# Linear attention, routed experts and a dense layer in one kernel: routing cut into four parts and shared between VectorE and GpSimd, tables of powers in PSUM, one score tile with one mask

## The chip, the cores and the metric

One Trainium2 chip, one of its cores. The metric is device time in microseconds (us) of one launch, the median of three runs. A change of 0.2% of it is about 1.6 us. The engines are named as in the profile: PE is TensorE's matmul, PEld its weight load, DVE is VectorE, ACT is ScalarE, POOL is GpSimd, SP is the engine whose queue issues most DMAs.

## The reference, cut to what matters

Three stages, all in float32, for 4 sequences of 768 tokens (3072 tokens), 8 heads of 48 numbers (384 numbers a token):

```python
# 1 attention with a decaying state, per sequence and head
for t in range(S):
    cur = outer(u * k[t], v[t])
    y[t] = r[t] @ (state + cur)
    state = w[:, None] * state + outer(k[t], v[t])
# 2 each token goes to one of 8 experts, the one with the largest logit
logits = x @ w_gate                       # x is y, a row for each token
e = argmax(logits); gate = softmax(logits)[e]
x2 = gate * (relu(x @ w1[e]) @ w2[e])     # w1 384x1024, w2 1024x384
# 3 a dense layer for all tokens
h = x2 @ w_in                             # 384x2048
out = max(0.01 * h, h) @ w_out            # 2048x384
```

## The kernel before, in words

**Attention** runs in 24 units of 128 tokens (6 chunks of each of the 4 sequences), in a loop over steps `n` that is a software pipeline written out by hand (`attention`, from L322). Each engine runs its own list of instructions in the order of the program, so the order of the calls in a step is the order of the work on each engine. In step n:

- SP's queue loads the transposed k and r (`kT`, `rT`) and v of unit n+2, and k and r of unit n+3; steps 4 to 11 also issue one DMA of zeros each (`zero_region`) into the region of one expert in the DRAM buffer `xs`, which has 3072 rows for each expert.
- PE makes the scores of unit n (`scores`, L432) into two PSUM tiles `pa0` and `pa1`, each with two buffers; then the values and the state update of unit n-1 (`values`, L462 and L468; `update`, L453, into one PSUM bank `pu`), then `rows` of unit n-2 (L507), which turns the result back to token rows and gives the router's logits.
- DVE reduces the logits of unit n-3 (L515), adds `pu` to the state (L498), scales kT and rT of unit n+2 by tables of powers of the decay (`prep_T`, L389 with `iG` and L390 with `G`, both tables in SBUF), copies the scores under a mask into `A` (`masked`, L438, two instructions), and reduces a product for unit n+2 (L411).
- ACT fills the diagonal of `A` for unit n+1 (L421, eight instructions), evicts `py` (L477) and `pr` (L519), and decays the state (L487).
- POOL forms k times a table (L402) and r times k times u of unit n+3 (L397, L398).

**Routing** comes once for each group of four units, in two lumps: `route1` at step 4g+6 (the largest logit, the difference to it, the one-hot choice; DVE, with one exponential on ACT), then at step 4g+7 `route1b` (the gate) and `route2` (positions, by small matmuls with a triangle of ones; then DVE). All of it but the exponential, the matmuls and one memset is on DVE. An indirect DMA on POOL (`scatter`, L690) then writes each unit's 128 rows of 388 numbers to `xs`; the steps are listed in `SCATTER_AT`. At step 16 `choose_first` picks the expert that leads so far; at step 17 SP reads that choice into a register (`load_first`, L233) and issues the first piece of the expert's weights, and one more piece in each step after it.

**The experts** follow in nine windows of columns: the leading expert has a window of 256 rows, known from the first 16 units, and one of `CAPS[0]` - 256 rows, and the other seven one each. `load_rows` (L793) fetches the rows of a window from `xs`, `turn` (L809) transposes them, and each window has 144 matmuls (L832 and L857). Weights and activations are split into a high and a low part of a packed float32 type, and three products stand for one. Steps of this stage are numbered again from 0; in the first three the routing of the last four units is done (`meanwhile`). **The dense layer** has L944 and L963, and ends in an indirect DMA by token number.

An off-line fallback (`leftovers`) runs when a flag says that a count went over its cap. With the reference's inputs the leading expert has 409 tokens and the smallest 348, so that no flag is raised.

Of the kernel before, what the change touches and what calls it, by code (L numbers as in the profile page):

```python
# [33 lines left out]

WARM = 5
ZERO_AT = 4
# [3 lines left out]
EARLYM = 0  # L40
# [16 lines left out]
PAD = 292  # L57
assert sum(CAPS) <= S * B + PAD
ZR = 512
LP = 116  # L60
RW = 388
# [9 lines left out]
class Kernel:  # L71
# [71 lines left out]
    def late_tables(self, one, keep, const):  # L143
# [15 lines left out]
        nc.vector.tensor_copy(out=self.rev, in_=ri)  # L159

    def later_tables(self, one, const):
# [5 lines left out]
        nc.vector.tensor_copy(out=self.carry, in_=ci)  # L167
        self.region = c([1, E], F32, "region")
        nc.vector.tensor_copy(out=self.region, in_=ci[0:1, :])
# [4 lines left out]
        nc.vector.tensor_copy(out=self.place, in_=ei)  # L174
        self.caps = c([1, E], F32, "caps")
        for k in range(E):
            nc.vector.memset(self.caps[:, k : k + 1], float(CAPS[k]))
# [24 lines left out]
    def counts(self, keep, name):  # L202
        nc = self.nc
        f = lambda nm: keep.tile([1, E], F32, name=f"{name}_{nm}")
        cnt, key = f("cnt"), f("key")
        nc.vector.tensor_tensor(out=cnt, in0=self.carry[0:1, :], in1=self.region, op=ALU.subtract)

        nc.vector.scalar_tensor_tensor(
            out=key, in0=cnt, scalar=16.0, in1=self.rev[0:1, :], op0=ALU.mult, op1=ALU.add
        )  # L210
        return cnt, key

    def choose_first(self, keep):

        nc = self.nc
        cnt, key = self.counts(keep, "half")
        mx = keep.tile([1, 1], F32, name="half_mx")
        x = keep.tile([1, E], F32, name="half_x")
        idf = keep.tile([1, 1], F32, name="half_id")
        self.lead = keep.tile([1, E], F32, name="lead")  # L220
        self.first_i = keep.tile([1, 1], I32, name="first_i")
        nc.vector.tensor_reduce(out=mx, in_=key, axis=AX.X, op=ALU.max)
        nc.vector.tensor_scalar(out=self.lead, in0=key, scalar1=mx, scalar2=None, op0=ALU.is_equal)
        nc.vector.tensor_tensor(out=x, in0=self.lead, in1=self.place, op=ALU.mult)
        nc.vector.tensor_reduce(out=idf, in_=x, axis=AX.X, op=ALU.add)
        nc.vector.tensor_scalar(out=idf, in0=idf, scalar1=float(E - 1), scalar2=0.0, op0=ALU.min, op1=ALU.max)
        nc.vector.tensor_copy(out=self.first_i, in_=idf)
# [10 lines left out]
    def early_flag(self, keep):  # L238

        nc = self.nc  # L240
        cnt, _ = self.counts(keep, "early")
        nc.vector.tensor_tensor(out=cnt, in0=cnt, in1=self.lead, op=ALU.mult)
        n = keep.tile([1, 1], F32, name="early_n")
        nc.vector.tensor_reduce(out=n, in_=cnt, axis=AX.X, op=ALU.add)
        nc.vector.tensor_scalar(out=n, in0=n, scalar1=float(EARLY), scalar2=None, op0=ALU.is_lt)
        self.redo = n
# [45 lines left out]
    def flag_rows(self, small, tmp):  # L292
# [3 lines left out]
        cap, over, n = (small.tile([1, w], F32, name=f"f{i}") for i, w in enumerate((E, E, 1)))  # L296
# [8 lines left out]
        V.tensor_tensor(out=n, in0=f[:, 1:2], in1=self.redo, op=ALU.max)  # L305
        V.tensor_tensor(out=f[:, 0:1], in0=f[:, 0:1], in1=n, op=ALU.max)

        V.tensor_tensor(out=n, in0=f[:, 1:2], in1=self.far, op=ALU.max)
# [6 lines left out]
    def attention(self, xs, clist, extra, const, route):  # L315
        nc, tc, a = self.nc, self.tc, self.a
        with ExitStack() as ctx:
# [8 lines left out]

            def load(n, names=("kT", "rT", "k", "r", "v")):
                if n >= NU:
                    return
                d = st.setdefault(n, {})  # L330
                for nm in names:
                    shp, bufs = {
                        "kT": ([HP, NP, P], 4), "rT": ([HP, NP, P], 4), "k": ([P, DM], 4), "r": ([P, DM], 4),
                        "v": ([P, DM], 5),
                    }[nm]
                    d[nm] = ld.tile(shp, F32, tag=nm, name=nm, bufs=bufs)
                    nc.sync.dma_start(out=d[nm], in_=a[nm][n])
# [45 lines left out]
            def prep_T(n):  # L383
# [5 lines left out]
                nc.vector.tensor_tensor(out=d["K"], in0=d["kT"], in1=self.iG, op=ALU.mult)  # L389
                nc.vector.tensor_tensor(out=d["R"], in0=d["rT"], in1=self.G, op=ALU.mult)  # L390
# [951 lines left out]
```

## Time and profile before

| | |
|---|---|
| median of 3 runs | 816.93 us (815.88 to 817.71) |
| profiled execution, its own time | 813.28 us |
| its span, first to last instruction | 811.5 us |
| PE busy | 770.8 us (95%) |
| DVE busy | 504.4 us (62%) |
| ACT busy | 378.1 us (47%) |
| POOL busy | 196.6 us (24%) |
| mean granted TensorE clock | 0.965 of full |

The page divides the span into 40 slices. In its line for the TensorE clock five of the first seven slices are below nine tenths, and from the eighth to the last but one none is; its line for VectorE has 7 to 9 in most of the first seven slices and 3 to 5 in the second half. Shares of the whole span therefore say little of the attention stage, which is the first fifth of it. The stage is read from the timeline of each engine and from sums over stretches.

### The profile page before, as it was taken

How to read it: one execution, taken by the hardware profiler on the slowest of the kernel's cores; microseconds unless marked ns; L12 is line 12 of the kernel's file. 1: busy time of each engine (PE TensorE's matmuls, PEld its weight loads, DVE VectorE, ACT ScalarE, POOL GpSimd, SP SyncE). 2: the span in 40 equal slices, each digit the busy share in tenths (PEclk: the TensorE clock that was granted, in tenths of full speed). 3: DMA queues.
4: the chain of work that ended last, by engine and by line, in shares of the span. 5: the costliest groups of instructions: out<-in, count | busy, mean ns of one | idle time of the engine just before them, and what ended most of it. 6: DMA issues, size and time to landing. Idle time of an engine off the chain costs nothing.

```text
span 811.5 us, 13201 instructions
## 1 busy us (share of the span) xinstructions
PE 770.8 (95%) x4906; PEld 706.2 (87%) x4906; DVE 504.4 (62%) x913; ACT 378.1 (47%) x800; POOL 196.6 (24%) x175
## 2 busy tenths in 40 slices
PE   7789878998999999999999999999999999999994
PEld 4678767898999999999899999999999999999993
DVE  7798998856889899989975443333333343343331
ACT  5586857735544555556444433342343333233321
POOL 5755673460212222223210020020010002002001
PEclk8698977999999999999999999999999999999998
DMA  8999739547886677677731010010000001001001
GB/s 216 283 326 287 233 128 269 163 144 211 223 241 199 196 226 242 206 224 208 172 123 49 0 40 1 1 40 0 1 30 11 0 1 40 1 1 39 1 1 43
DMA packets 55178, 97.80 MB, mean 121 GB/s; under 512 B 12189, under 2 KB 33089, under 8 KB 55105
## 3 DMA queue, kind: packets, MB, share of 16 engines
q1 hardware_dynamic: 52033, 87.38, 37.8%
q0 software_dynamic: 3072, 9.49, 3.2%
q8 instruction: 40, 0.66, 0.4%
q14 instruction: 33, 0.27, 0.1%
HBM read 74.69 MB, written 22.19 MB: 119 GB/s over the span
## 4 chain that ended last, share of the span: by engine, by line
PE 72%; DVE 10%; issue 9%; DMA 6%; POOL 1%; ACT 1%; SPq 0%; POOLq 0%; DVEq 0%; ACTq 0%
PE ph L944 21%; PE o L963 20%; PE y L857 11%; PE ph L832 11%; PE pr L507 2%; PE py L468 2%; DMA rT<-in_rT 2%; PE pa L432 2%; PE py L462 2%; DVE A L438 1%; DMA v<-in_v 1%; DMA raw<-in_wE 1%; DVE R L390 1%; PE pt L809 1%; DMA u_row<-in_u 1%
## 5 line engine op out<-in xcount | busy, mean ns | idle before, releaser
L963 PE MATMUL o<-c,gg 128*128 128x384 f32 x1152 | 216.3, 336 | 0.0
L944 PE MATMUL ph<-x,c 128*128 128x512 f32 x864 | 215.7, 394 | 0.7 <-DVE x L923 0.7
L963 PEld LDWEIGHTS o<-c,gg 128*128 128x128 f32 x1152 | 203.7, 188 | 8.8
L944 PEld LDWEIGHTS ph<-x,c 128*128 128x128 f32 x864 | 160.4, 188 | 30.4 <-DVE x L923 1.1
L950 DVE TENSOR_TENSOR s<-s,ph 128x512 f32<-128x512 f32 x96 | 66.0, 688 | 166.9 <-ACT s L949 166.9
L949 ACT ACTIVATE s<-ph 128x512 f32<-128x512 f32 x96 | 57.3, 597 | 173.9 <-PE ph L944 170.6
L857 PE MATMUL y<-hh,c 128*128 128x256 f32 (+7 forms) x648 | 123.2, 334 | 3.1 <-ACT hh L837 2.3
L832 PE MATMUL ph<-xe,c 128*128 128x256 f32 (+7 forms) x648 | 123.3, 335 | 0.6 <-DVE xe L813 0.6
L857 PEld LDWEIGHTS y<-hh,c 128*128 128x128 f32 x648 | 109.9, 188 | 6.4 <-ACT hh L837 2.5
L731 POOL TENSOR_TENSOR c<-raw,c 128x768 fp32r<-128x768 f32 x32 | 61.2, 1913 | 209.8 <-ACT c L722 142.1
L832 PEld LDWEIGHTS ph<-xe,c 128*128 128x128 f32 x648 | 108.3, 188 | 2.7 <-DVE xe L813 1.0
L953 DVE TENSOR_TENSOR gg<-s,gg 128x512 fp32r<-128x512 f32 x96 | 66.5, 692 | 67.0 <-ACT gg L952 67.0
L976 POOL DMA_INDIRECT out<-z,cl x24 | 24.3, 1014 | 322.6 <-ACT z L975 318.6
L952 ACT ACTIVATE gg<-s 128x512 fp32r<-128x512 f32 x96 | 60.7, 632 | 82.9 <-DVE s L950 82.9
L722 ACT ACTIVATE c<-raw 128x768 fp32r<-128x768 f32 x80 | 67.1, 838 | 14.2 <-DMA raw<-in_wE 14.1
L837 ACT ACTIVATE hh<-ph 128x256 fp32r<-128x256 f32 (+7 forms) x72 | 34.6, 481 | 65.2 <-PE ph L832 65.1
L421 ACT ACTIVATE A<-ident,av 128x128 f32<-128x128 f32 x192 | 58.5, 390 | 2.2 <-DVE av L411 2.1
L731 DVE TENSOR_TENSOR c<-raw,c 128x768 fp32r<-128x768 f32 x48 | 47.5, 989 | 17.7 <-ACT c L722 17.4
L778 DVE SCALAR_TENSOR_TENSOR t<-raw,t 128x384 f32<-128x384 uint32 x32 | 42.4, 1324 | 1.1
L838 DVE SCALAR_TENSOR_TENSOR hh<-ph,hh 128x256 fp32r<-128x256 f32 (+7 forms) x72 | 38.8, 540 | 4.4 <-ACT hh L837 4.3
L468 PE MATMUL py<-A,v 128*48 128x128 f32 x384 | 34.3, 318 | 6.7 <-DVE A L438 6.6
L468 PEld LDWEIGHTS py<-A,v 128*48 128x48 f32 x384 | 25.6, 143 | 12.1 <-DVE A L438 3.5
(167 smaller groups left out, 738.2 us busy)
## 6 DMA issues: line engine op xcount, KB each, us to landing
raw<-in_wE SPq DMA_DIRECT2D x64, 384.0 KB, 4.2
raw<-in_w2nd SPq DMA_DIRECT2D x32, 384.0 KB, 4.6
xs<-z SPq DMA_DIRECT2D x8, 776.0 KB
w2f<-t SPq DMA_DIRECT2D x32, 192.0 KB, 4.0
raw<-w2f SPq DMA_DIRECT2D x16, 384.0 KB, 3.5
kT<-in_kT SPq DMA_DIRECT2D x24, 224.0 KB, 6.3
rT<-in_rT SPq DMA_DIRECT2D x24, 224.0 KB, 5.2
k<-in_k SPq DMA_DIRECT2D x24, 192.0 KB, 7.2
```

The source lines that it names most:

```text
L421: nc.scalar.activation(out=d["A"][:, h % 2, h // 2, :], in_=self.ident, func=AF.Copy, scale=d["av"][:, h : h + 1],)
L468: nc.tensor.matmul(py[64 * i : 64 * i + D, p, :], d["v"][:, (2 * p + i) * D : (2 * p + i + 1) * D], d["A"][:, i, p, :], start=(c == 0 and ...
L722: self.nc.scalar.activation(out=w[:, 0, c], in_=t, func=AF.Copy)
L731: eng.tensor_tensor(out=w[:, 1, c], in0=t, in1=w[:, 0, c].bitcast(F32), op=ALU.subtract)
L832: nc.tensor.matmul(ph[:, :cap], w[:, wl, c * 512 + o : c * 512 + o + P], self.xT[i][:, xl, c, :cap], start=(c == 0 and n == 0), stop=(c == ...
L857: nc.tensor.matmul(self.y[i][m][:, :cap], w[:, wl, o : o + P], t[:, xl, :cap], start=(f == 0 and n == 0), stop=(f == FF // P - 1 and n == 2),)
L944: nc.tensor.matmul(ph, w[:, wl, c * 512 + off : c * 512 + off + P], x2[b][:, xl, c, :], start=(c == 0 and i == 0), stop=(c == KD - 1 and i ...
L949: nc.scalar.activation(out=s, in_=ph, func=AF.Copy, scale=0.01)
L950: nc.vector.tensor_tensor(out=s, in0=s, in1=ph, op=ALU.max)
L952: nc.scalar.activation(out=t[:, 0, :], in_=s, func=AF.Copy)
L953: nc.vector.tensor_tensor(out=t[:, 1, :], in0=s, in1=t[:, 0, :].bitcast(F32), op=ALU.subtract)
L963: nc.tensor.matmul(o[b][k][:, :DM], t[:, gl, k * P : (k + 1) * P], w[:, wl, (f % 4) * DM : (f % 4 + 1) * DM], start=(f == 0 and i == 0), s ...
```

## The change

- `CAPS[0]` goes from 512 to 480, so the second window has 224 columns in place of 256; the zeros are written to rows 256 to 479 of each expert's region in place of rows 0 to 511, from step 3 on in place of step 4. `RW` goes from 388 to 386.
- Loads of kT and rT for units 4 and later leave out the 16 filler partitions: two DMAs of 48 partitions in place of one of 112. In a step, kT, rT, k and r are issued ahead of v.
- The tables `G` and `iG` are copied into PSUM at step 1 and used from there for units 4 and later.
- The scores of a unit go to one PSUM tile of two banks with one buffer, and one `copy_predicated` takes them. It stands ahead of `prep_T` in every step (before, behind it in all steps but 0).
- Routing of a group is cut into four parts in four successive steps. DVE keeps the reductions and what reads PSUM; the rest is on POOL, with the exponential and the matmuls where they were. `choose_first` is cut into three parts in steps 16 to 18, the early flag into two.
- The choice is read by SP at step 19, behind the loads of kT, rT, k and r and ahead of those of v; three weight pieces follow at once, the others in steps 21 to 24. Two of five low halves of pieces go to POOL.
- The last stage's token numbers are clamped by one VectorE instruction.

```diff
-ZERO_AT = 4
+ZERO_AT = 3
+POWERS_AT = 2
 SCATTER_AT = {
-    **{13 + 2 * g + i: [(g, 2 * i), (g, 2 * i + 1)] for g in (0, 1) for i in (0, 1)},
-    **{17 + u: [(2, u)] for u in range(3)},
-    20: [(2, 3), (3, 0)],
-    21: [(3, 1), (3, 2), (3, 3)],
-    23: [(4, u) for u in range(4)],
+    11: [(0, 0)],
...
+    20: [(2, 2), (2, 3)],
+    21: [(3, u) for u in range(4)],
+    24: [(4, u) for u in range(4)],
 }
-CAPS = (512, 456, 432, 416, 400, 392, 384, 372)
+CAPS = (480, 456, 432, 416, 400, 392, 384, 372)
...
+                    if nm in turned:
+                        d[nm] = t = turned[nm][n % TB]
+                        for q in [slice(0, HP)] if n < TB else [slice(0, D), slice(64, 64 + D)]:
+                            nc.sync.dma_start(out=t[q], in_=a[nm][n, q])
+                        continue
...
+            powers = [ps1.tile([HP, NP, P], F32, tag=nm, name=nm) for nm in ("pG", "piG")]
...
+                G, iG = powers if n >= POWERS_AT + 2 else (self.G, self.iG)
+                nc.vector.tensor_tensor(out=d["K"], in0=d["kT"], in1=iG, op=ALU.mult)
+                nc.vector.tensor_tensor(out=d["R"], in0=d["rT"], in1=G, op=ALU.mult)
...
-                d["pa"] = pa = [ps.tile([P, NP, P], F32, tag=f"pa{i}", name=f"pa{i}") for i in range(2)]
+                d["pa"] = pa = ps1.tile([P, 2, NP, P], F32, tag="pa", name="pa")
...
-                for i in range(2):
-                    nc.vector.copy_predicated(out=st[n]["A"][:, i], mask=mask, data=st[n]["pa"][i])
+                flat = lambda t: t.rearrange("s i p t -> s (i p) t")
+                nc.vector.copy_predicated(out=flat(st[n]["A"]), mask=mask, data=flat(st[n]["pa"]))
...
+                if n == 19:
+                    first_weights()
+                for m in ahead:
+                    load(m, ("v",))
...
+                for part in range(3, -1, -1):
+                    g, u = divmod(n - 3 - part, B)
+                    if u == B - 1 and 0 <= g < NC - 1:
...
+                        self.route(part, g, route, nc.gpsimd, bank)
...
+        if part == 0:
+            V.tensor_reduce(out=d["mx"], in_=d["lg"], axis=AX.X, op=ALU.max)
+            eng.tensor_tensor(out=d["df"], in0=d["lg"], in1=be(d["mx"]), op=ALU.subtract)
...
+                eng.tensor_scalar(out=d["eq"], in0=d["df"], scalar1=0.0, scalar2=None, op0=ALU.is_equal)
+                eng.tensor_tensor(out=d["eq"], in0=d["eq"], in1=rev, op=ALU.mult)
+            nc.scalar.activation(out=d["ex"][:, :, 0:E], in_=d["df"], func=AF.Exp)
+        elif part == 1:
+            V.tensor_reduce(out=d["m2"], in_=d["eq"], axis=AX.X, op=ALU.max)
+            V.tensor_reduce(out=se, in_=d["ex"], axis=AX.X, op=ALU.add)
+            V.reciprocal(out=d["rows"][:, :, DM], in_=se)
...
+                eng.tensor_tensor(out=d["df"], in0=d["eq"], in1=be(d["m2"]), op=ALU.subtract)
+                eng.tensor_scalar(out=d["oh"], in0=d["df"], scalar1=0.0, scalar2=None, op0=ALU.is_equal)
+            eng.tensor_copy(
+                out=d["rows"].bitcast(I32)[:, :, DM + 1], in_=self.tokid[:, B * g : B * (g + 1)]
+            )
+        elif part == 2:
...
+            V.tensor_tensor(out=self.carry, in0=self.carry, in1=pk[:, B, :], op=ALU.add)
+            eng.tensor_tensor(out=d["pos"], in0=d["pos"], in1=oh, op=ALU.mult)
+        else:
+                V.tensor_reduce(out=d["ix"], in_=d["pos"], axis=AX.X, op=ALU.add)
...
+    def first_weights():
+        k.load_first()
+        for i in range(3):
+            k.piece_load(i)
+
     def extra(n):
-        if n == 17:
-            k.load_first()
-        if 17 <= n < 17 + 8:
-            k.piece_load(n - 17)
-        if 20 <= n < 20 + 5:
-            k.piece_low(n - 20)
-        if 19 <= n < 19 + 5:
-            k.piece_high(n - 19)
+        for i in {20: (0,), 21: (1,), 22: (2,), 23: (3, 4)}.get(n, ()):
+            k.piece_high(i)
+        for i in {21: (0,), 22: (1,), 23: (2,), 24: (3, 4)}.get(n, ()):
+            k.piece_low(i, nc.gpsimd if i in (1, 3) else None)
+        for i in {21: (3,), 22: (4,), 23: (5,), 24: (6, 7)}.get(n, ()):
+            k.piece_load(i)
```

## Rows read from the trace of the kernel before

**Rows 1.** Sums by stretch: busy us of each engine (instructions), clock, DMA, GB/s.
```profile
34.51:77.50 42.99, 38.30 (x449) 34.36 (x448) 38.52 (x87) 32.69 (x103) 25.16 (x30) 0.84 1.00 310
72.92:77.50 4.58, 4.58 (x65) 4.17 (x64) 4.21 (x8) 4.41 (x15) 2.96 (x4) 1.00 1.04 326
77.50:137.36 59.86, 48.66 (x602) 43.10 (x601) 54.12 (x121) 39.94 (x129) 36.86 (x39) 0.88 0.72 211
...
192.41:811.47 619.06, 606.15 (x3182) 561.56 (x3182) 348.04 (x533) 254.61 (x439) 85.56 (x56) 0.99 0.30 88
```

**Rows 2.** TensorE's timeline, start and us: score blocks of steps 4, 8, 9, 11, 20, 23; transposes.
```profile
34.51 1.16 PE L432 MATMUL pa<-R,K 48*128 48x128 f32 x16
...
60.25 2.08 PE L432 MATMUL pa<-R,K 48*128 48x128 f32 x16
...
68.33 1.16 PE L432 MATMUL pa<-R,K 48*128 48x128 f32 x16
...
77.50 1.16 PE L432 MATMUL pa<-R,K 48*128 48x128 f32 x16
...
137.36 2.08 PE L432 MATMUL pa<-R,K 48*128 48x128 f32 x16
...
153.12 1.16 PE L432 MATMUL pa<-R,K 48*128 48x128 f32 x16
...
157.59 0.88 PE L809 MATMUL pt<-ident,erows 128*128 128x128 f32 x6
```

**Rows 3.** Waits, 34.51 to 137.36: who waited for whom, us, times, longest.
```profile
PE pu L453 <- DVE St L498: 12.1, 6, 4.5
```

**Rows 4.** VectorE's timeline: start, us, line, operation and tiles.
```profile
49.79 0.70 DVE L498 TENSOR_TENSOR St<-St,pu 48x192 f32<-48x192 f32 x2
...
74.16 1.45 DVE L389 TENSOR_TENSOR K<-kT,iG 112x512 f32<-112x512 f32 x1
...
77.93 0.18 DVE L632 TENSOR_REDUCE mx<-lg 128x4 f32<-128x32 f32 x1
...
79.77 1.15 DVE L647 CAST oh<-oh 128x32 bf16<-128x32 f32 x1
...
84.57 0.17 DVE L653 TENSOR_REDUCE se<-ex 128x4 f32<-128x32 f32 x1
...
87.47 0.17 DVE L685 CAST ix<-ixf 128x4 int32<-128x4 f32 x1
...
88.39 0.69 DVE L389 TENSOR_TENSOR K<-kT,iG 112x512 f32<-112x512 f32 x1
```

**Rows 5.** GpSimd's timeline: products of two tiles, then two scatters.
```profile
49.64 1.00 POOL L398 TENSOR_TENSOR rk<-rk,u_row 128x384 f32<-128x384 f32 x1
...
74.06 0.99 POOL L398 TENSOR_TENSOR rk<-rk,u_row 128x384 f32<-128x384 f32 x1
...
148.60 0.97 POOL L690 DMA_INDIRECT xs<-rows,ix  x1 [0.30 <-ACT A L421]
149.88 1.11 POOL L690 DMA_INDIRECT xs<-rows,ix  x1 [0.30 <-ACT c L722]
```

**Rows 6.** Groups by line, 34.51 to 137.36: the masked copy, busy us, mean ns, idle.
```profile
L438 DVE COPY_PREDICATED A<-strict,pa 128x512 f32<-128x512 int32 x34 | 22.9, 725 | 0.5
```

**Rows 7.** DMA issues: the zeros, count and size of one.
```profile
xs<-z SPq DMA_DIRECT2D x8, 776.0 KB
```

**Rows 8.** The DMA queue's own waits, 100 to 130.
```profile
SPq L233 <- DVE lg L515: 9.5, 1, 9.5
```

**Rows 9.** SP's timeline: the load of the first window's rows.
```profile
154.44 0.38 SPq L793 DMA_DIRECT2D erows<-xs  x1
```

**Rows 10.** TensorE's timeline in the second window, two blocks of nine matmuls.
```profile
193.47 1.24 PE L832 MATMUL ph<-xe,c 128*128 128x256 f32 x9
194.54 1.24 PE L857 MATMUL y<-hh,c 128*128 128x256 f32 x9
```

**Rows 11.** The chain that ended last: matmuls of plain float32, 104 columns.
```profile
152.00 1.07 PE pr L507 x8
```

More of the change, by code (lines that the diff above doesn't have):

```diff
@@ L158, in late_tables @@
         self.rev = c([P, E], F32, "rev")
-        nc.vector.tensor_copy(out=self.rev, in_=ri)
+        nc.gpsimd.tensor_copy(out=self.rev, in_=ri)
+        self.ex = [r([P, B, E + 1], F32, f"ex{i}") for i in range(2)]
+        for x in self.ex:
+            nc.gpsimd.memset(x[:, :, E : E + 1], 1e-9)
     def later_tables(self, one, const):
@@ L211, in counts, with choose_first @@
         return cnt, key
[L213 to L227, printed above, removed]
+    def choose_first(self, keep, part):
+        V, G = self.nc.vector, self.nc.gpsimd
+        if part == 0:
+            f = lambda nm, w=1, dt=F32: keep.tile([1, w], dt, name=nm)
+            _, self.half_key = self.counts(keep, "half", G)
+            self.half_mx, self.half_x, self.half_id = f("half_mx"), f("half_x", E), f("half_id")
+            self.lead, self.first_i = f("lead", E), f("first_i", 1, I32)
+        elif part == 1:
+            V.tensor_reduce(out=self.half_mx, in_=self.half_key, axis=AX.X, op=ALU.max)
+            G.tensor_scalar(
+                out=self.lead, in0=self.half_key, scalar1=self.half_mx, scalar2=None, op0=ALU.is_equal
+            )
+            G.tensor_tensor(out=self.half_x, in0=self.lead, in1=self.place, op=ALU.mult)
+        else:
+            V.tensor_reduce(out=self.half_id, in_=self.half_x, axis=AX.X, op=ALU.add)
+            G.tensor_scalar(
+                out=self.first_i, in0=self.half_id, scalar1=float(E - 1), scalar2=0.0, op0=ALU.min, op1=ALU.max
+            )
@@ L236, in index, with early_flag @@
         )
[L238 to L246, printed above, removed]
+    def early_flag(self, keep, part):
+        V, G = self.nc.vector, self.nc.gpsimd
+        if part == 0:
+            self.early_cnt, _ = self.counts(keep, "early", G)
+            G.tensor_tensor(out=self.early_cnt, in0=self.early_cnt, in1=self.lead, op=ALU.mult)
+        else:
+            self.redo = n = keep.tile([1, 1], F32, name="early_n")
+            V.tensor_reduce(out=n, in_=self.early_cnt, axis=AX.X, op=ALU.add)
+            V.tensor_scalar(out=n, in0=n, scalar1=float(EARLY), scalar2=None, op0=ALU.is_lt)
     def order(self, small, tmp):
@@ L295, in flag_rows @@
         f = self.flags
-        cap, over, n = (small.tile([1, w], F32, name=f"f{i}") for i, w in enumerate((E, E, 1)))
+        cap, over, n, low = (small.tile([1, w], F32, name=f"f{i}") for i, w in enumerate((E, E, 1, 1)))
         m = tmp.tile([1, E, E], F32, tag="t0", name="fm")
@@ L325, in attention @@
             st = {}
+            turned = {nm: [one.tile([HP, NP, P], F32, name=f"{nm}{i}") for i in range(TB)] for nm in ("kT", "rT")}
             def load(n, names=("kT", "rT", "k", "r", "v")):
@@ L558, in attention @@
                 if n == NU:
-                    self.turn(0, ps, ("pa0", "pa1", "pa0"))
+                    both = ps1.tile([P, 2, 512], F32, tag="pa", name="pa")
+                    third = ps.tile([P, 512], F32, tag="rt", name="pt")
+                    self.turn(0, None, (both[:, 0], both[:, 1], third))
                 if 0 <= n - 1 < NU:
@@ L729, in piece_low @@
         c = slice(half * (CW // 2), (half + 1) * (CW // 2))
-        eng = nc.gpsimd if i >= 16 and i % 2 else nc.vector
+        eng = eng or (nc.gpsimd if i >= 16 and i % 2 else nc.vector)
         eng.tensor_tensor(out=w[:, 1, c], in0=t, in1=w[:, 0, c].bitcast(F32), op=ALU.subtract)
@@ L806, in turn @@
             x = self.xT[i]
-            pt = ps.tile([P, 512], F32, tag=tag if isinstance(tag, str) else tag[c], name="pt")
+            pt = ps.tile([P, 512], F32, tag=tag, name="pt") if ps else tag[c]
             for j in range(nj):
@@ L934, in second_part @@
         nc.sync.dma_start(out=cl, in_=clist[0:NT, :].rearrange("(j p) c -> p j c", p=P))
+        to = pools["small"].tile([P, NT // P], I32, name="to")
         g, o, z4 = {}, {}, {}
```

203 lines of the change are left out of this document (99 added, 104 removed).

## The prediction

> **What bounds the kernel now.** I read the stretch sums first, to see where TensorE is not full. From 192.4 us to the end it is busy 606 of 619 us at full clock [rows 1], so nothing that spares VectorE or GpSimd is worth anything there. The attention stage is different: 38.3 of 43.0 us, then 48.7 of 59.9, at granted clocks of 0.84 and 0.88, while VectorE is busy 38.5 and 54.1 us [rows 1].
>
> Next the start of each step, taken from its score block [rows 2]. Step 4 starts at 34.51, step 11 at 77.50, step 20 at 137.36 and step 23 at 153.12. The step from 72.92 to 77.50 is an undisturbed one, 4.58 us, and there PE is busy throughout, ACT 4.41, DVE 4.21, POOL 2.96 [rows 1]. The mean is 43.0/7 = 6.14 us in steps 4 to 10 and 59.9/9 = 6.65 in 11 to 19. So some 10.9 + 18.6 us are lost against the undisturbed step, and the question is to what. Four things show.
>
> VectorE's routing lumps. The first half of a group runs from the reduction at 77.93 to the end of the cast at 80.92, seven instructions, 3.0 us; the second from 84.57 to 87.64, nine, 3.1 us [rows 4]. In that time the state addition is not made, and TensorE's next update waits for it: 12.1 us in six waits [rows 3].
>
> The waits inside them. The product K takes 0.69 us alone (88.39) and 1.45 when a GpSimd product runs from 74.06 to 75.05; the cast at 79.77 takes 1.15, another cast 0.17 [rows 4, 5]. But the state addition, whose second input lies in PSUM, takes 0.70 for the usual two instructions while GpSimd's product of 49.64 runs [rows 4, 5]. I read this as two engines taking turns at SBUF inputs, from which a PSUM input is exempt.
>
> DMA. From 34.5 to 77.5 its share is 1.00 at 310 GB/s, so 13.3 MB [rows 1], of which the zeros are 8 x 776 KB = 6.36 MB [rows 7].
>
> The register read at step 17: SP waits 9.5 us for the choice [rows 8], and every load behind it waits too; step 20 starts late. Spells of idleness are paid for once more. The blocks at 60.25 and 137.36 take 2.08 us in place of 1.16, the lower of the two clock levels (1.2 GHz in place of 2.4) after waits of up to 4.5 us [rows 3]; the step from 60.25 lasts 8.08 us [rows 2], 3.5 more than undisturbed.
>
> **The change, part by part.** Routing on VectorE: of 16 instructions and 6.1 us a group, seven stay (four reductions, a reciprocal, two additions from PSUM, all on 128x32 or less). At the 0.17 to 0.18 us of rows 4 that is 1.25 us, in four steps, so at most 0.6 in one. An undisturbed step leaves VectorE 4.58 - 4.21 = 0.37 us [rows 1], and it gains more below; the lumps leave the path.
>
> K and R from PSUM: 0.69 us, not shown for these shapes. The bounds are 0.69 (no turn-taking, as the addition at 49.79) and 1.45 (turn-taking as now) [rows 4, 5]; I take 0.69, because the addition has the same mix of inputs.
>
> One mask: 725 ns a copy now [rows 6], so two are 1.45 at most; one of double width is between that and 0.73 us. I take 1.3; it is no bound of the step either way. Its place ahead of `prep_T` matters more: now a late kT holds the mask and with it the values of the step before; then only later work waits. What replaces it: the score tile has one buffer, so scores n+1 wait for mask n. Between two score blocks TensorE has about 4.58 - 1.16 = 3.4 us of other work [rows 1, 2], which covers the mask with 2 us to spare; without that cover a step would grow by what the mask is late.
>
> GpSimd gets seven small instructions a group, four tables, and waits for the reductions. A step of its own is now 2.96 us [rows 1] and a scatter every 1.28 [rows 5], with one scatter a step 4.24. No small product stands in the trace. Bounds: nothing, and 1.0 us as the 128x384 ones [rows 5]; at a twelfth of their width I take 0.25, so 0.44 a step and 4.7 us, just over the undisturbed step. At 1.0 it is 4.24 + 7/4 = 6.0. Queued behind a waiting small instruction are GpSimd's next products, two steps ahead of their use, and behind the exponential ACT's next evictions. I take 4.85 us for steps 11 to 19. For elementwise work with two inputs the Trainium skill ("GPSIMD Engine Reference", 4.1 Engine selection) advises VectorE, as GpSimd is about twice as slow, and so speaks against this move. By it the small instructions would be some 0.35 us, GpSimd's step 4.85, and nine steps 1.6 us longer in all; rows 4 and 5 have no like pair to test it.
>
> DMA: the zeros fall to 8 x 224 x 386 x 4 bytes = 2.77 MB, 3.6 MB less, and each later kT and rT by a seventh (0.46 MB over seven units). At 310 GB/s [rows 1] 13.3 - 4.1 = 9.2 MB are 30 us for seven steps, 4.3 each: DMA stops being the bound but has little to spare. SP issues two more DMAs a step; at 0.38 us [rows 9], eight are 3.0, hidden in 4.6. I take 4.8 us for steps 4 to 10; if the transfers keep the pace down it is up to 5.4.
>
> The register read moves behind the loads of units 22 and 23, except their v, which is used four steps later: the 9.5 us go. The tables to PSUM are two ACT copies at step 1, under DMA waits. Table casts moved to GpSimd are under 2 us and lie in the above.
>
> Steps 0 to 3 wait for data, but the mask no longer waits for rT of unit 3. I estimate step 4 at 30 in place of 34.5, bounds 28.5 and 34.5.
>
> Something is late next. The scatters of group 3 now all come in step 21, as the last routing part does. VectorE ends its part some 4.4 us into step 21, that is 2 x 4.58 - 4.4 = 4.8 us ahead of step 23; four scatters at 1.28 are 5.1; the last landed 3.45 us after its end (150.99 to the load at 154.44), and the transposes followed the load by 3.15 [rows 2, 5, 9]. That gives step 23 + 6.9 us, against 157.59 - 153.12 = 4.5 now: 2.4 us, bounds 0 (if GpSimd is early) and 4.
>
> The second window: 256 columns take 1.07/9 = 119 ns [rows 10]; by width 224 take 104, so 15 x 144 = 2.1 us; I count the part behind the stall there, 1.3, bounds 0 and 2.1. The last group's routing on VectorE loses four instructions of 0.2: 0.8 us.
>
> The sum. Step 4: -4.5. Steps 4 to 10: 7 x 4.8 = 33.6, so -9.4. Steps 11 to 19: 9 x 4.85 = 43.7, so -16.2. Steps 20 to 22: 13.8 for 15.8, -2.0. One spell of the low clock left, +3.5. Tail +2.4 - 1.3 - 0.8 = +0.3. In all -28.3: the profiled execution's 813.3 us become 785.0, and the median, 3.65 us above that execution, 816.9 becomes 788.6.
>
> **The rivals.** *Smaller gain: another engine sets the step.* GpSimd at 6.0 in steps 11 to 19 gives 10 us back: 799; DMA at 5.4 in steps 4 to 10 4 us: 793; both 803. For it: DMA at 1.00, ACT at 4.41 of 4.58 and now waiting for GpSimd's difference. Against: four engines fit in one undisturbed step already.
>
> *Nothing to see.* If the turn-taking did not end and VectorE's relief only moved the wait to GpSimd's instructions, the steps would stay near 6.4 and only window, start and zeros would show, some 0 to 5 us: 812 to 817. Against it stands the addition at 49.79.
>
> *Slower: the narrow window.* No packed matmul under 256 columns is in the trace. The nearest narrow ones are plain float32 of 104 columns, two matmuls a product: 8 in 1.07 us, 0.268 us a product [rows 11], 2.6 ns a column where the packed type has 0.46. If 224 columns fell to that rate, 576 ns, the 144 would cost 144 x (576 - 119) = 66 us: 816.9 - 27.0 + 65.8 = 856. It turns the gain into a loss from 119 + 187 = 306 ns a matmul. For it: every window so far has 256 or more. Against: nothing else than width changes.
>
> *Larger gain.* Steps at 4.58 throughout, no spell, no late transposes: 788.6 - 1.5 - 2.4 - 3.5 - 2.4 = 779.
>
> **How the numbers follow.** Forecast (780 to 796) 0.60, smaller gain (796 to 811) 0.19, larger 0.08, nothing to see 0.04 (0.01 of it faster, 0.03 within 0.2%), slower 0.09. The range 776 to 806 leaves out the last two and a little of each side. 0.2% (1.6 us) is about what a measurement tells from no change. Faster 0.88, same 0.03, slower 0.09.
>
> **What would show it.** Right: score blocks every 4.6 to 5 us from step 4 on with hardly one at 2.08; K and R at 0.69 throughout; step 11 near 64 and step 23 near 120 us; hardly a wait of `pu` for the state; transposes of the first window later after step 23 than 4.5 us; nine matmuls of 224 columns in 0.94 us. Wrong: a GpSimd step over 5 us with ACT or VectorE waiting for its small instructions; score blocks that wait for the mask; a DMA share still at 1.00 with late kT; 224 columns at over 119 ns.

## The result and the profile after

The changed kernel takes 804.96 us (median of 4 runs, 803.77 to 808.06) beside 816.40 for the kernel before. The ratio on record is 0.9899, 95% interval 0.9859 to 0.9940; the two medians by themselves give 0.986. The profiled execution took 805.47 us with a span of 803.8. It is faster, but by 11.4 us by the medians where 28.3 were forecast.

The terms of the sum can be read one by one from the starts of the steps and of the windows. The last column is experiment `e1`, told below.

| stretch, us | before | forecast | after | e1 |
|---|---|---|---|---|
| start to step 4 | 34.5 | 30.0 | 29.6 | 31.0 |
| steps 4 to 10 | 43.0 | 33.6 | 32.6 | 31.9 |
| steps 11 to 19 | 59.9 | 43.7 | **52.8** | 43.1 |
| steps 20 to 22 | 15.8 | 13.8 | **22.4** | 19.0 |
| step 23 to the first expert matmul | 8.1 | 10.5 | **15.5** | 15.8 |
| from there to the third window | 41.0 | 38.9 | **43.8** | 43.4 |
| from there to the end | 609.3 | 609.3 | 607.1 | 605.9 |
| low-clock spell, not placed | - | 3.5 | - | - |
| span | 811.5 | 783.3 | 803.8 | 789.9 |

Each column is one profiled execution; that of e1 took 791.62 us, 1.8 under the median of its runs. The changed kernel's 20.5 us over the forecast span are 9.1 + 8.6 + 5.0 + 4.9 in the four rows in bold, less 0.4 + 1.0 + 2.2 + 3.5 in the others.

TensorE's timeline of the changed kernel (start and us) answers to [rows 2]. Step 11 starts at 62.13, near the 64 that was forecast. Step 16 is the first that stalls: 15.0 us to the next block where an undisturbed step has 4.6. Step 20 takes 13.8. TensorE's first wait in step 16 is 7.69 us, and what follows it runs at 1.2 GHz (eight `py` in 2.05 us for 1.13, a granted clock of 0.56 from 95.02 to 101.19).

```profile
62.13 1.16 PE L470 MATMUL pa<-R,K 48*128 48x128 f32 x16
...
86.17 1.16 PE L470 MATMUL pa<-R,K 48*128 48x128 f32 x16
...
95.02 2.05 PE L500 MATMUL py<-R,St 112*112 112x128 f32 x8 [7.69 <-ACT xT L515]
...
101.19 1.16 PE L470 MATMUL pa<-R,K 48*128 48x128 f32 x16
...
114.94 1.16 PE L470 MATMUL pa<-R,K 48*128 48x128 f32 x16
...
128.75 1.16 PE L470 MATMUL pa<-R,K 48*128 48x128 f32 x16
...
137.32 1.16 PE L470 MATMUL pa<-R,K 48*128 48x128 f32 x16
```

The sums by stretch answer to [rows 1]. From step 4 to 11 TensorE is at full clock and the DMA share has left 1.00; an undisturbed step, from 77.00, has TensorE and ScalarE full, GpSimd and VectorE at nine tenths. In step 16 none of them is busy for more than 8.83 of 15.02 us.

```profile
29.57:62.13 32.56, 31.50 (x448) 28.57 (x448) 27.86 (x58) 32.28 (x103) 22.50 (x39) 1.00 0.89 265
...
77.00:81.59 4.59, 4.59 (x66) 4.18 (x65) 4.11 (x9) 4.59 (x16) 4.33 (x5) 1.00 0.88 278
86.17:101.19 15.02, 7.33 (x74) 6.75 (x73) 4.34 (x11) 8.83 (x28) 7.86 (x11) 0.66 0.72 215
```

ScalarE's timeline shows who stood still. `rows`, the eviction of unit 12 at step 15, waits 7.25 us for a DMA that reads `rows`, and the diagonals, `xT` and the decay stand behind it; four steps later unit 16 waits 6.55. In the waits of the stretch the two are one row, 13.8 us.

```profile
84.19 0.23 ACT L698 ACTIVATE ex<-df 128x32 f32<-128x32 f32 x1 [1.47 <-POOL df L689]
91.67 0.49 ACT L557 ACTIVATE rows<-pr 128x384 f32<-128x384 f32 x1 [7.25 <-DMA xs<-rows,ix]
...
94.39 0.58 ACT L515 ACTIVATE xT<-py 112x512 f32<-112x512 f32 x1
...
119.46 0.49 ACT L557 ACTIVATE rows<-pr 128x384 f32<-128x384 f32 x1 [6.55 <-DMA xs<-rows,ix]
```

The rows of a group lie in one tile of four units, and there are three such buffers. Unit 12 opens group 3, which takes the buffer of group 0; its first eviction waits until the last of group 0's four scatters has been read out of it. That scatter is listed for step 14, one to a step; GpSimd starts it at 85.37 and ScalarE goes on at 91.67. GpSimd's timeline, which answers to [rows 5], shows it behind small routing instructions, 1.5 us from 83.91 on:

```profile
83.91 0.24 POOL L689 TENSOR_TENSOR df<-lg,mx 128x32 f32<-128x32 f32 x1
84.25 0.30 POOL L696 TENSOR_SCALAR eq<-df 128x32 f32<-128x32 f32 x1
...
85.37 1.06 POOL L739 DMA_INDIRECT xs<-rows,ix  x1 [0.48 <-issue]
```

ScalarE stands at the eviction from 84.42, where the Exp ends, which is ahead of the scatter's start; by these times most of the wait would be there without the small instructions too (an estimate). In the kernel before, the last scatter of group 0 stands in step 14 as well. It starts at 101.66 there, and the same eviction comes 5.3 us later, behind VectorE's routing lump and not behind the buffer. GpSimd, then ScalarE:

```profile
101.66 0.97 POOL L690 DMA_INDIRECT xs<-rows,ix  x1 [0.30 <-issue]
106.97 0.49 ACT L519 ACTIVATE rows<-pr 128x384 f32<-128x384 f32 x1 [2.05 <-DVE lg L515]
```

VectorE's timeline answers to [rows 4]: K and R take 0.66 to 0.69 us each with their tables in PSUM, also beside GpSimd's products (R at 81.00 beside one from 80.92 to 81.93), the one mask 1.31 to 1.34, and the 9.21 us in front of the state addition are the stall on ScalarE, no longer VectorE's own.

```profile
81.00 0.68 DVE L428 TENSOR_TENSOR R<-rT,pG 112x512 f32<-112x512 f32 x1
...
96.12 0.72 DVE L536 TENSOR_TENSOR St<-St,pu 48x192 f32<-48x192 f32 x2 [9.21 <-ACT St L525]
96.87 1.31 DVE L476 COPY_PREDICATED A<-strict,pa 128x1024 f32<-128x1024 int32 x1
```

At the end of the stage two more queues are seen. GpSimd makes the difference of group 4, the last that is routed in the loop, at 140.76, behind four scatters and the low half of a weight piece (1.84 us). ScalarE's Exp waits for it, and then the fifth piece (145.41) waits for its load with the evictions of the transposed rows behind it.

```profile
138.00 0.97 POOL L739 DMA_INDIRECT xs<-rows,ix  x1 [0.30 <-issue]
138.99 1.84 POOL L780 TENSOR_TENSOR c<-raw,c 128x768 fp32r<-128x768 f32 x1
140.76 0.98 POOL L689 TENSOR_TENSOR df<-lg,mx 128x32 f32<-128x32 f32 x1
```

```profile
141.78 0.23 ACT L698 ACTIVATE ex<-df 128x32 f32<-128x32 f32 x1 [3.49 <-POOL df L689]
...
145.41 0.84 ACT L771 ACTIVATE c<-raw 128x768 fp32r<-128x768 f32 x1 [1.70 <-DMA raw<-in_wE]
146.16 0.36 ACT L861 ACTIVATE xe<-pa 128x256 fp32r<-128x256 f32 x1
```

TensorE there, and in the second window: the transposes start at step 23 + 6.5 us and then wait again, and nine matmuls of 224 columns take 1.01 us from start to start. A wait for a weight piece stops the window, as before, and the clock is low after it: ScalarE's copy of the piece waits 5.97 us for its load, up to 183.63 (5.09 in the kernel before), with the eviction of `hh` behind it. ScalarE's sum of these waits from 155 to 200 us, then TensorE's timeline:

```profile
ACT c L771 <- DMA raw<-in_wE: 10.0, 3, 6.0
```

```profile
143.84 0.41 PE L858 MATMUL pa<-ident,erows 128*128 128x128 f32 x2 [2.22 <-DMA erows<-xs]
147.03 0.69 PE L858 MATMUL pa<-ident,erows 128*128 128x128 f32 x2 [2.79 <-DVE xe L862]
...
152.85 1.32 PE L881 MATMUL ph<-xe,c 128*128 128x256 f32 x9
...
178.15 1.17 PE L881 MATMUL ph<-xe,c 128*128 128x224 f32 x9
179.16 1.16 PE L906 MATMUL y<-hh,c 128*128 128x224 f32 x9
...
184.77 0.37 PE L906 MATMUL y<-hh,c 128*128 128x224 f32 x1 [3.45 <-ACT hh L886]
185.82 2.05 PE L906 MATMUL y<-hh,c 128*128 128x224 f32 x8 [0.68 <-DVE hh L887]
```

### The profile page after: what moved, and what is told of

The parts are those of the page before. It is cut to its first block, busy times and chain, and to the rows that moved or that the text cites. A ratio compares the mean times of both kernels' runs of the same rounds, so it can differ in the third digit from the quotient of the medians.

```text
span 803.8 us, 13222 instructions
## 1 busy us (share of the span) xinstructions
PE 754.8 (94%) x4906; PEld 695.3 (87%) x4906; DVE 470.1 (58%) x830; ACT 378.2 (47%) x802; POOL 205.7 (26%) x222
## 4 chain that ended last, share of the span: by engine, by line
PE 75%; DMA 8%; DVE 6%; ACT 4%; POOL 3%; issue 2%; SPq 0%; POOLq 0%; DVEq 0%; ACTq 0%
PE o L1014 25%; PE ph L995 25%; PE y L906 11%; PE ph L881 10%; ACT A L459 2%; DMA erows<-xs 2%; DMA raw<-in_wE 2%; DMA xs<-rows,ix 2%; PE py L506 1%; PE pt L858 1%; PE py L500 1%; DMA r<-in_r 1%; DVE c L780 1%; DVE t L810 1%; DMA u_row<-in_u 1%
## 5 line engine op out<-in xcount | busy, mean ns | idle before, releaser
L906 PE MATMUL y<-hh,c 128*128 128x256 f32 (+8 forms) x648 | 123.5, 335 | 4.5 <-ACT hh L886 3.7
L881 PE MATMUL ph<-xe,c 128*128 128x256 f32 (+8 forms) x648 | 124.0, 337 | 0.7 <-DVE xe L862 0.7
L780 POOL TENSOR_TENSOR c<-raw,c 128x768 fp32r<-128x768 f32 x34 | 64.7, 1904 | 212.6 <-ACT c L771 152.8
L1027 POOL DMA_INDIRECT out<-z,to x24 | 24.2, 1009 | 320.6 <-ACT z L1026 302.3
L771 ACT ACTIVATE c<-raw 128x768 fp32r<-128x768 f32 x80 | 67.2, 840 | 15.6 <-DMA raw<-in_wE 15.5
L886 ACT ACTIVATE hh<-ph 128x256 fp32r<-128x256 f32 (+8 forms) x72 | 34.5, 479 | 65.6 <-PE ph L881 65.4
L887 DVE SCALAR_TENSOR_TENSOR hh<-ph,hh 128x256 fp32r<-128x256 f32 (+8 forms) x72 | 38.7, 537 | 4.6 <-ACT hh L886 4.5
L500 PE MATMUL py<-R,St 112*112 112x128 f32 x160 | 25.2, 306 | 15.2 <-ACT xT L515 15.2
L470 PE MATMUL pa<-R,K 48*128 48x128 f32 x384 | 29.4, 295 | 8.1 <-DVE A L476 7.9
```

The lines of the kernel that those rows point to most:

```text
L771: self.nc.scalar.activation(out=w[:, 0, c], in_=t, func=AF.Copy)
L780: eng.tensor_tensor(out=w[:, 1, c], in0=t, in1=w[:, 0, c].bitcast(F32), op=ALU.subtract)
L881: nc.tensor.matmul(ph[:, :cap], w[:, wl, c * 512 + o : c * 512 + o + P], self.xT[i][:, xl, c, :cap], start=(c == 0 and n == 0), stop=(c == ...
L906: nc.tensor.matmul(self.y[i][m][:, :cap], w[:, wl, o : o + P], t[:, xl, :cap], start=(f == 0 and n == 0), stop=(f == FF // P - 1 and n == 2),)
```

## Experiments

The kernel before gave medians of 814.9, 817.4 and 813.8 us in the three sets, so sets are compared by their ratios to it. Theory A of the first expectations is that the three buffers of rows, freed late by scatters that come one to a step, cost the two stalls.

**e1: the rows in one tile, released unit by unit.** On the changed kernel; the same bytes, but an eviction now depends on the scatter of its own unit's place only.

```diff
-                "rows": route.tile([P, B, RW], F32, tag="rows", name="rows", bufs=3),
+            if not hasattr(self, "ring"):
+                self.ring = route.tile([P, 3 * B, RW], F32, name="rows", bufs=1)
+            at = B * (g % 3)
+                "rows": self.ring[:, at : at + B, :],
```

> The changed kernel with one tile of twelve unit slots for the token rows in place of three tiles of four units, the same bytes: the eviction of a unit's rows then waits for the scatter of the one unit whose slot it takes, not for all four of that group. Theory A (the two long steps, 16 and 20, come from that wait on ACT): both fall from 15.0 and 13.8 us to under 5.5, step 23 starts near 118 us in place of 137.3, and the time is 785 to 791. Rival B (GpSimd is a step behind and sets the pace; the wait is only where it shows): ACT's exponential or VectorE's reductions wait for GpSimd instead, the two steps stay over 8 us, and the time is 798 to 804. Rival C (the single score buffer): nothing moves, 803 to 807.

793.43 us, ratio 0.9731 (0.9714 to 0.9748): far from the changed kernel, and a little short of what A expected (785 to 791). On ScalarE unit 12's eviction no longer waits, though the Exp of group 2 ahead of it still waits for GpSimd. It is made at 85.10, 1.0 us before group 0's last scatter starts (86.14), so that it no longer depends on that scatter:

```profile
84.97 0.23 ACT L701 ACTIVATE ex<-df 128x32 f32<-128x32 f32 x1 [1.34 <-POOL df L692]
85.10 0.47 ACT L557 ACTIVATE rows<-pr 128x384 f32<-128x384 f32 x1
...
106.54 0.23 ACT L701 ACTIVATE ex<-df 128x32 f32<-128x32 f32 x1 [4.09 <-POOL df L692]
```

TensorE's blocks show step 16 at 5.1 us instead of 15.0, and step 20 still at 10.4:

```profile
87.08 1.16 PE L470 MATMUL pa<-R,K 48*128 48x128 f32 x16
92.15 1.16 PE L470 MATMUL pa<-R,K 48*128 48x128 f32 x16
...
105.91 1.16 PE L470 MATMUL pa<-R,K 48*128 48x128 f32 x16
116.28 1.16 PE L470 MATMUL pa<-R,K 48*128 48x128 f32 x16
...
124.86 1.16 PE L470 MATMUL pa<-R,K 48*128 48x128 f32 x16
```

Steps 11 to 19 now take 43.1 us, against 43.7 in the prediction's sum. Theory A holds for them; 3.4 us of the 8.6 in excess in steps 20 to 22 go too. The 5.2 that are left are in step 20, where A expected under 5.5 us: ScalarE's Exp waits 4.09 us there, TensorE 2.94 behind it, and the granted clock of the step is 0.67. The prediction's sum had 3.5 us for one such spell, without a place; with them step 23 was due at 124.6, and it starts at 124.86. The tail has another cause.

**e2: the scatters two to a step again, and earlier**, on the changed kernel, its group buffers kept. Group 0 is scattered by step 11 in place of 14 (as in the kernel before), group 1 by step 15 in place of 18.

```diff
-    11: [(0, 0)],
-    12: [(0, 1)],
-    13: [(0, 2)],
-    14: [(0, 3)],
-    15: [(1, 0)],
-    16: [(1, 1)],
-    17: [(1, 2)],
-    18: [(1, 3), (2, 0)],
+    10: [(0, 0), (0, 1)],
+    11: [(0, 2), (0, 3)],
+    14: [(1, 0), (1, 1)],
+    15: [(1, 2), (1, 3)],
+    18: [(2, 0)],
```

> The changed kernel with the scatters of groups 0 and 1 two to a step and earlier (group 0 in steps 10 and 11, group 1 in 14 and 15), nothing else. Theory A: the slots are free when unit 12 and unit 16 need them, both long steps go, 786 to 793. Rival B: GpSimd has two scatters in a step and falls further behind, the time is 803 or more. Rival C: 803 to 807.

794.08 us, ratio 0.9735 (0.9719 to 0.9752): in the total the same cure from the other side. The eviction that waited 7.25 us follows the Exp ahead of it at once. By stretch it is not the same: steps 11 to 19 take 48.8 us (43.1 in e1), step 12 7.1 and step 16 still 8.8 of them, with the wait of 2.51 us for GpSimd's difference shown here; steps 20 to 22 take 14.4 (19.0 in e1), and step 23 starts at 126.3 (124.9).

```profile
89.39 0.23 ACT L695 ACTIVATE ex<-df 128x32 f32<-128x32 f32 x1 [2.51 <-POOL df L686]
89.55 0.49 ACT L554 ACTIVATE rows<-pr 128x384 f32<-128x384 f32 x1
```

**e5: the kernel before with the tile of e1.**

> The kernel before with the same twelve unit slots. Theory A (before the change the routing lumps on VectorE came later than the slots were free, so the ring cost nothing): within 1.5 us of the kernel before. Rival D (the ring already set step 15, which took 11.2 us): 4 to 8 us less.

814.49 us, ratio 1.0003 (0.9975 to 1.0031). In the kernel before the ring cost nothing: it scattered group 0 by step 14 too, but two to a step and without the small instructions ahead, and where its evictions wait, it is for VectorE's reduction (22.5 us in 15 waits from 30 to 155 us), never for a scatter. The stall is made by the change.

**e3: the fifth weight piece later**, on the changed kernel; **e4** is the same on e1.

```diff
-        for i in {20: (0,), 21: (1,), 22: (2,), 23: (3, 4)}.get(n, ()):
+        for i in {20: (0,), 21: (1,), 22: (2,), 23: (3,), 24: (4,)}.get(n, ()):
             k.piece_high(i)
```

> The changed kernel with the high half of weight piece 4 taken one step later (24 in place of 23), behind the first window's transposes on ACT. From the score block of step 23 to the first expert matmul it is 15.5 us in the changed kernel. Theory A (ACT sits in front of that piece, whose load comes behind the late load of the first window's rows): 12 to 13.5 us, and the time 1 to 3.5 us lower, 801.5 to 804. Rival (the late rows alone set it): within 1 us of the changed kernel.

803.39 us, ratio 0.9859 (0.9828 to 0.9891), which overlaps the changed kernel's own interval. The wait of 1.70 us ahead of the evictions is gone, the second pair of transposes waits 0.93 in place of 2.79, and the first expert matmul comes 14.3 us after step 23's scores instead of 15.5. A cause of 1 us, not of 5.

> The ring by unit, and the copy of the high half of the fifth piece of weights issued a step later (step 24 for 23). In the run with the ring by unit ScalarE waits 2.01 us for this piece's load with the two evictions of the transposed rows behind it, and the second pair of transposes waits 3.12 us. Theory: 1.5 to 2.5 us, time 790.5 to 792. Rival: the transposes wait for the rows' load anyway and the order changes nothing, time 793 to 794.

Inconclusive: the four runs take 791.43, 802.40, 803.41 and 804.35 us, and no ratio is on record. In the profiled one (802.40) the first expert matmul comes at 139.6, 1.1 earlier than in e1, but the first window is broken: two small VectorE instructions (L293 and L294), which take 0.15 and 0.20 us in e1, take six each, side by side, and TensorE waits 3.75 us behind them for `hh` and goes on at the lower clock (17 matmuls in 4.00).

```profile
155.65 6.12 DVE L293 TENSOR_SCALAR idsf<-idsf 1x8 f32<-1x8 f32 x1
```

What held the two instructions the trace does not say, and the cause stays open.

**e6: the routing parts on VectorE; e7: the Exp a step later.** Both on e1, to see whether the remaining waits of ScalarE for GpSimd's difference (2.61, 1.34, 4.09, 3.49 us) are worth their length.

```diff
-                        self.route(part, g, route, nc.gpsimd, bank)
+                        self.route(part, g, route, nc.vector, bank)
```

> The ring by unit plus the four routing parts wholly on VectorE (the same instructions otherwise; the masked maximum becomes one instruction instead of two). In the run with the ring by unit ScalarE's Exp of each group waits for GpSimd's difference, which stands in GpSimd's queue behind a scatter and the products: 2.61, 1.34, 4.09 and 3.49 us for the four groups, 11.5 together, and ScalarE's rows, diagonals and decays stand behind it. Theory G (these waits are on the path, VectorE has room): all but some 3 us of VectorE's added work comes back, span 781 to 785, time 782 to 787. Rival V (VectorE is as full as GpSimd, what moves to it costs what the waits gave): time 791 to 795. Rival T (only the wait of the last group counts, as the others are caught up): time 789 to 791.

792.50 us (787.90 to 798.12), ratio 0.9698 (0.9624 to 0.9773): not to be told from e1. The Exp's waits shrink to 1.5 us in all and step 20 falls from 10.4 to 4.8, but VectorE now carries all of the routing, and steps 11 to 19 grow from 43.1 to 45.4 us. Its timeline shows where: an instruction of 0.18 us, both of its inputs in SBUF, takes 0.8 to 2.2 when it meets GpSimd's work.

```profile
74.85 2.21 DVE L734 TENSOR_TENSOR pos<-pos,oh 128x32 f32<-128x32 f32 x1
...
85.53 1.00 DVE L692 TENSOR_TENSOR df<-lg,mx 128x32 f32<-128x32 f32 x1
...
95.56 0.18 DVE L734 TENSOR_TENSOR pos<-pos,oh 128x32 f32<-128x32 f32 x1
```

```diff
-            nc.scalar.activation(out=d["ex"][:, :, 0:E], in_=d["df"], func=AF.Exp)
         elif part == 1:
+            nc.scalar.activation(out=d["ex"][:, :, 0:E], in_=d["df"], func=AF.Exp)
```

> The ring by unit, and ScalarE's Exp of a group issued at the start of the second routing part, a step later; GpSimd keeps its share of the routing. Theory Q (what costs is ScalarE's in-order wait for the difference, not GpSimd's load): the waits of 2.61, 1.34, 4.09 and 3.49 us go, time 783 to 788. Rival L (in the steps with routing GpSimd itself has more than a step of work, and the next thing that waits for it, VectorE's reduce of the products or the diagonal, takes the wait over): time 790 to 794.

794.67 us, ratio 0.9726 (0.9678 to 0.9775): nearest to rival L. The waits for GpSimd come back elsewhere, at the reduction of its products (0.6 us in e1) and at the matmuls of the positions (none in e1). Sums of waits, 64 to 126 us:

```profile
DVE av L449 <- POOL rk L436: 4.1, 4, 1.3
...
PE pu L718 <- POOL oh L711: 3.5, 2, 2.6
```

So the routing's place is worth nothing measurable on e1: GpSimd was busy 51.7 of 60.9 us there (64.0 to 124.9) and stood 4.3 more at the issue of scatters; in e6 VectorE is busy 55.9 and ScalarE 55.2 of 61.5.

**e8: the tables of powers in SBUF**, on e1.

```diff
-POWERS_AT = 2
+POWERS_AT = 99
```

> The ring by unit, and the two products K and R read their tables from SBUF in all steps, as in the kernel before; the rest of the change stays. Theory P (the tables in PSUM are what made the plain step 4.6 us and less): K and R go back from 0.67 us each towards 1.15 to 1.45 beside GpSimd's work, 0.6 to 0.9 us a step for some 20 steps, time 805 to 812. Rival M (VectorE has slack, the one masked instruction and its place carry the gain): under 4 us, time 793 to 797.

805.25 us, ratio 0.9840 (0.9784 to 0.9896): 9 us by the ratio, 12 by the medians, against e1. VectorE's groups from 30 to 140 us (count; busy us, mean ns; idle before): K and R together take 2.72 us a step for 1.35.

```profile
L427 DVE TENSOR_TENSOR K<-kT,iG 112x512 f32<-112x512 f32 x19 | 27.5, 1447 | 0.1
L428 DVE TENSOR_TENSOR R<-rT,G 112x512 f32<-112x512 f32 x19 | 24.2, 1276 | 0.0
```

**e9: the mask in two instructions, behind K, R and the diagonal**, on e1 with its one score buffer.

```diff
-                if n < NU:
+                if n == 0:
                     masked(n)
...
                 prep_diag(n + 1)
+                if 0 < n < NU:
+                    masked(n)
...
-                nc.vector.copy_predicated(out=flat(st[n]["A"]), mask=mask, data=flat(st[n]["pa"]))
+                for i in range(2):
+                    nc.vector.copy_predicated(out=st[n]["A"][:, i], mask=mask, data=st[n]["pa"][:, i])
```

> The ring by unit, and the scores masked by two instructions of 512 columns behind K, R and the diagonal, as in the kernel before; the scores keep their one tile of two banks with one buffer. The prediction took the one instruction (1.3 us for 2 x 0.73) as no bound and its place as what matters. Theory (the place is worth something because the values of a step, and now also the next scores, wait for the mask): 5 to 10 us longer than the ring by unit, time 798 to 804. Rival (TensorE has 3.4 us of other work that covers a mask 1.3 us later): 793 to 796.

799.86 us, ratio 0.9834 (0.9820 to 0.9847). Both sides are right, each in its steps. From step 7 to 19 the blocks come every 4.6 to 4.8 us, so the cover holds. In the first steps it doesn't: VectorE's copy of the state waits for that step's own update, K, R (0.69 and 0.68 us) and the mask come behind it, and the next scores wait for the mask. Step 4 starts at 35.2 us for e1's 31.0, and steps 4 to 10 take 39.7 for 31.9. The two copies of 512 columns take 1.32 to 1.33 us together, as the one of 1024 does, so it is the place that costs and not the second instruction. VectorE, then TensorE:

```profile
39.35 0.72 DVE L538 COPY St<-pu 48x192 f32<-48x192 f32 x2 [3.80 <-PE pu L491]
...
41.31 1.33 DVE L476 COPY_PREDICATED A<-strict,pa 128x512 f32<-128x512 int32 x2
```

```profile
42.78 2.08 PE L470 MATMUL pa<-R,K 48*128 48x128 f32 x16 [2.41 <-DVE A L476]
```

**e10: the transposes of the first window behind step 24's own matmuls; e11: that and the Exp of e7.** Both on e1. In step 24 the call moves from ahead of values and update to behind `rows_out(n - 3)`:

```diff
-                if n == NU:
...
-                    self.turn(0, None, (both[:, 0], both[:, 1], third))
                 if 0 <= n - 1 < NU:
...
                 rows_out(n - 3)
+                if n == NU:
...
+                    self.turn(0, None, (both[:, 0], both[:, 1], third))
```

> The ring by unit, and in step 24 TensorE's transposes of the first window are queued behind the values, the update and the rows of that step in place of ahead of them (ScalarE's eviction of the rows goes ahead of those of the transposes too). In the run with the ring by unit TensorE waits 2.10 and 3.12 us at the transposes and then makes 5 us of values and rows at the lower clock. Theory: those run under the waits, 3 to 5 us come back, time 788 to 790.5. Rival (the experts wait for the rows' load, the evictions and the weights in any case): under 1 us, time 792.5 to 794.

793.10 us, ratio 0.9737 (0.9718 to 0.9757): no gain over e1. The first expert matmul comes 1.9 us earlier, 138.70 for 140.64, and 1.1 of them are left at the third window. The second window stops for a weight piece at the same distance: it goes on 32.7 us after the first expert matmul here, 32.5 in e1, 33.0 in the changed kernel, 31.2 in the kernel before. From there to the third window it then needs 11.6 us for e1's 10.9. From the third window to the end the profiled executions take 608.4 and 605.9 us; that difference, which hides the 1.1, lies where the edit changes nothing, and its cause is open.

```profile
138.70 2.25 PE L884 MATMUL ph<-xe,c 128*128 128x256 f32 x9 [0.53 <-DVE xe L865]
...
171.42 2.05 PE L909 MATMUL y<-hh,c 128*128 128x224 f32 x8 [0.49 <-DVE hh L890]
```

> As the run with the late transposes, and the Exp a step later too. The Exp alone brought nothing in the loop (794.67), but at the end ScalarE's wait of 3.49 us for it stands ahead of the rows and the transposed rows. Theory: another 1.5 to 3.5 us than the late transposes alone, time 785 to 788.5. Rival: the load of the rows at step 23 + 3.3 us sets the time, nothing more, time as the late transposes alone within 1 us.

790.93 us, ratio 0.9716 (0.9702 to 0.9730): the fastest of its set, by about 2 us, but its interval overlaps those of e1 and e10, so that a gain is not shown. The first expert matmul is at 136.8, 3.8 us earlier than in e1; 2.5 of them are left at the third window.

**e12: the second window at 256 columns again**, on e1 (`CAPS[0]` 512, `PAD` 292, `LP` 116; the zeros follow).

> The ring by unit with the second window back at 256 columns (cap 512, and the zeros to row 512). In the trace nine matmuls of 224 columns took 1.01 us against 1.07 for 256. Theory: 144 matmuls x 7 ns = 1.0 us at most, and some of it hidden by the wait for weights, so window two 0 to 1 us longer in the trace, time 793 to 795. Rival of the prediction (224 columns fall out of the fast rate): the second window would be shorter with 256, time under 790.

795.91 us, ratio 0.9779 (0.9764 to 0.9793). The window's part behind its stall takes 11.3 us for 10.9 in e1; the ratio has 4 us, which lie in no one place: of the 4.4 us between the two profiled spans, 1.3 are ahead of the first expert matmul, 0.8 from there to the third window and 2.2 behind it. The narrow window is a small gain and no loss.

## Why the prediction fell short

**The step that failed** is the scatters of steps 11 to 19, which I took as a load on GpSimd alone. I counted what a scatter a step costs GpSimd (4.24 us, 4.85 a step with the rest) and, in the tail, when the last one lands; I did not ask who waits for the buffer that a scatter reads. Nothing in the rows showed it, since the kernel before has no such wait, but three buffers of four units and the listed steps were in the code. The price was 9.1 us in steps 11 to 19 and 3.4 of the 8.6 in steps 20 to 22; e1 and e2 give it back each in its own way, 11 us of the total by the medians, and e5 shows that it was not there before. The load itself was right: in the undisturbed step from 77.00 GpSimd is busy 4.33 us, scatter included. The other 5.2 of the 8.6 are, going by e1, the low-clock spell that the sum had at 3.5 us without a place.

**The tail was mis-sized.** The transposes at step 23 + 6.5 (forecast 6.9) are right, but the first expert matmul comes 7.4 us later after step 23 than before, not 2.4. Behind late transposes stand ScalarE's Exp (3.49 us for a difference behind four scatters and a piece of weights on GpSimd), the fifth piece, and then a whole step of matmuls at 1.2 GHz (granted clock 0.60 from 147.00 to 152.85). Taking parts of it away (e3, e10, e11) brings the first expert matmul 1 to 4.5 us nearer to step 23. Of what e10 and e11 gain on e1 there, 1.9 and 3.8 us, 1.1 and 2.5 are left at the third window: the second window stops for a weight piece and goes on 32.5 to 33 us after that matmul in the changed kernel and in e1, e3, e10 and e11, with a slow stretch behind it. No run shows what the whole tail is worth.

**The second window**: 1.01 us for nine matmuls against 0.94 forecast and 1.07 before, 112 ns each: neither the width nor the slow rate of the rival. The 1.3 us did not come, as the clock after the stall is low for two groups of nine (2.05 and 1.89 us) where it was full before. From the first expert matmul to the third window the changed kernel takes 2.8 us more than the kernel before, 1.8 up to the end of the stall and 1.0 behind it.

**Right** were step 4 (29.6 for 30), steps 4 to 10 (32.6 for 33.6), K and R at 0.66 to 0.69 with PSUM tables, the end of the waits of `pu` for the state (0.5 us for 12.1), and, with the ring mended, steps 11 to 19 (43.1 for 43.7). The mask is 1.31 us for 1.3, but the two copies that it replaces took 1.35 together and not 1.45, so nearly nothing is saved on VectorE; its place pays, in e9, by the state copy of the first steps, not by a late kT. Of the rivals, "another engine sets the step" is half true: GpSimd's small instructions are cheap, 0.18 to 0.30 us, but ScalarE and VectorE wait for them in order. The measured 804.96 us lie in that rival's range (796 to 811) and not by its mechanism, a GpSimd step of 6.0 us. The 2.2 us by which the stretch behind the third window is shorter than before had no term in the sum; for the forecast they are luck.

For the rule that the prediction weighed (the Trainium skill, "GPSIMD Engine Reference", 4.1 Engine selection: about twice as slow as VectorE) these runs now have the pairs that rows 4 and 5 lacked. The product of 128x32 takes 0.24 us on GpSimd (101.57 in the changed kernel) and 0.18 on VectorE when it meets nothing (95.56 in e6); the low half of 128x768 takes 1.84 and 0.94 to 0.96 (one of the 15 on VectorE from 140 to 205 us took 1.83). The rule fits the wide instruction, the small one costs a third more. Against it, moved back to VectorE the small ones gave no time (e6).

## What to carry to other kernels

When a transfer out of a buffer is moved later or spread, ask first which write next takes that buffer, and count from the transfer's landing to that write in steps; with tiles of several units the first write of the next turn waits for the last reader. A stall of a buffer shows on an engine that has nothing to do with the change, because that engine works in order: look at what is ahead of it in its queue. Where four engines each fill over nine tenths of a step, moving small work between them gives little.

## What the runs showed of the hardware

- A second input in PSUM frees a VectorE instruction of GpSimd's turns wholly: 0.66 to 0.69 us in all 40 products with a table in PSUM, for means of 1.28 and 1.45 with the tables in SBUF (e8), beside the same products. Without it even an instruction of 0.18 us can take 2.21 (e6). That one began at 74.85 and ended just behind the second of two GpSimd products (75.05 to 76.05 and 76.01 to 77.00). The Trainium skill ("SBUF — State Buffer", SBUF: two separate sides) says that whichever of the two starts first keeps the shared ports for its whole instruction and the other is fully blocked; the 0.68 and 1.45 us agree. The 2.21 go further: the loser sat out two instructions in a row, though its recorded start is ahead of both; a scatter (74.01 to 75.02) ran on GpSimd at that time.
- A scatter of 128 rows holds its source for some time after GpSimd has gone on: it starts at 85.37, is 1.06 us long on GpSimd, and its buffer is free at 91.67. The ten scatters from 60 to 125 us took 3.9 to 6.2 us from issue to landing.
- Packed matmuls of 224 columns run at 112 ns and those of 256 at 119, so that a narrower window gains less than its width.
